# Retention and SwiGLU on one core: the second gate and val tile ahead of group 1's first pair, and the opening ordered anew

## The chip, the cores and the metric

The kernel runs on one core of a Trainium2 chip. The metric is device time in microseconds (us) of one execution, the median of three runs. Beside it stands one profiled execution; the rows below are read from that one, with times counted from the start of its span.

## The reference

Two steps are fused. The first is a block-wise linear attention with decay (a retention): inside a block the scores are masked by powers of a per-head factor, and between blocks a state is carried.

```python
for b in range(nb):
    intra = np.einsum('bhic,bhjc->bhij', qb, kb) * Dmask[None]
    intra = np.einsum('bhij,bhjd->bhid', intra, vb)
    inter = np.einsum('bhid,bhde->bhie', qb * lam_pow[None], kv_state)
    out[:, :, sl] = intra + inter
    kv_state = lam_block[None, :, None, None] * kv_state + np.einsum('bhsd,bhse->bhde', kb_dec, vb)
...
rms = np.sqrt(np.mean(x * x, axis=-1, keepdims=True) + 1e-06)
xn = x / rms * rms_g
g = xn @ w_gate
silu = g * (1.0 / (1.0 + np.exp(-g)))
return silu * (xn @ w_val) @ w_out
```

There are 4 batches of 768 tokens, 8 heads of 64, a model width of 512 and a hidden width of 1536, all in float32.

## The kernel before

**Tiling.** The 3072 tokens are cut into six groups of 512. A group's eight heads are four pairs; `Pair(m, p)` is pair p of group m. The 1536 hidden columns are twelve tiles of 128; `Hidden(m, f)` is group m's work on hidden tile f, and `Weights(f)` prepares the weights of that tile: the gate and val columns are loaded as 64-bit integers (`raw_gv`, 1 MB a tile), turned into float32 on ScalarE and VectorE (`lift`, `convert`), squared and summed for a scale (`square`, `norm`, `scale`), and split into a high and a low float16 half (`high`, `low`). The output rows of a tile come as `raw_o` (0.5 MB) by `lift_o` and `convert_o`. A gate or val product is twelve matmuls of 128x512: four of high weights by high x, four of low weights by high x, four of high weights by low x, and they can be issued a third at a time (`gate(0)`, `gate(1)`, `gate(2)`).

**The opening.** `ramp()` is a list of steps written out by hand. It runs group 0's and group 1's pairs (`p00` to `p13`), prepares weights `w0` to `w6` and does `h0` to `h5`, the first half of group 0's hidden tiles. Each engine works through its instructions in exactly the order in which the list issues them, and waits at the head of its queue for what an instruction needs. After `ramp()` a loop of units with a fixed pattern does the rest; it is the same before and after.

**What the steps are.** For a pair: `scores` (tile `pa`), `decay_a` (VectorE, the mask), `decay_k` (ScalarE), `decay_q` (GpSimd), `state_sums` (`pst`), `states`, `mix_chunks` and `mix_states` (both into `po`), `keep_output` (into `x`) and `keep_squares`. `row_sums` (`pss`) adds a group's squares; then `Norm` does `mean` (VectorE), `root` (GpSimd), `spread` (TensorE, tile `pr`), and for each quarter of the model width `scaled` (VectorE, tile `xn`), `high` (ScalarE) and `low`. The first gate matmul needs `high(0)` and the fourth `high(3)`. `busy(n)` issues n filler matmuls that nothing reads. `powers` makes the decay masks and, before the change, the powers `pw` by scans on VectorE.

**The loads.** All loads but one are issued by the sync engine (SP), in the order of the list `pending`, one entry for each `load_next()`. Pair tiles and gate-and-val tiles share four buffers (tag `in`), all four taken at first by `qkv_0_0` to `qkv_0_3`; weight tile 0 has a place of its own (`partial`). A load waits until a buffer is free. The gate and the val products have one accumulator each (`pg`, `pv`), which pairs of group 1 use too; a product can't begin until the last reader of what stood there is done.

Of the kernel before, what the change touches and what calls it, by code (L numbers as in the profile page):

```python
# [23 lines left out]
def retention_swiglu_kernel(  # L24
# [67 lines left out]
    def load_gv(f):  # L92
        if f == 0:

            t = partial.bitcast(I32).rearrange("p a (b w) -> p (a b) w", w=2)
            t = t.rearrange("p (k o) w -> p k o w", k=2)
            for i in range(2):
                nc.sync.dma_start(t[:, i], w_all[f, :, i])
        else:
            t = stage.tile([P, 2, G, 2], I32, tag="in", name=f"raw_gv_{f}", bufs=4)  # L100
            nc.sync.dma_start(t, w_all[f, :, 0:2])
            if f <= 2:
                load_o(f - 1)
        raws[f] = t
# [12 lines left out]
    pending = [(load_qkv, 1, 0), (load_gv, 1)]  # L117
# [37 lines left out]
    def powers(p, part):  # L155
        if part < 2:
            h = 2 * p + part
            nc.vector.tensor_tensor_scan(
                mask[:, h, :], lam_b[:, h : h + 1].broadcast_to([P, P]), ident, 0.0,
                ALU.mult, ALU.add,  # L160
            )
        else:
            nc.vector.tensor_tensor_scan(
                pw[:, p, :], lam_p[:, p : p + 1].broadcast_to([P, P]), zeros, 1.0,
                ALU.mult, ALU.add,
            )
# [23 lines left out]
    def scales_of(pmax):  # L190
        nc.vector.tensor_reduce(gmax, pmax[:, :P], axis=mybir.AxisListType.X, op=ALU.max)
        nc.vector.tensor_single_scalar(ge, gmax.bitcast(I32), 0x7F800000, op=ALU.bitwise_and)
        nc.vector.tensor_scalar_min(ge, ge, float(252 * EXP))
        nc.vector.tensor_scalar(sx.bitcast(I32), ge, -1.0, float(253 * EXP), ALU.mult, ALU.add)
        nc.vector.tensor_scalar(gs, gcol, sx, XS, ALU.mult, ALU.mult)
        nc.vector.tensor_scalar_add(cx.bitcast(I32), ge, float(EXP))
        nc.vector.tensor_scalar_mul(cx, cx, 1.0 / (XS * WS))
# [15 lines left out]

    zeros = wg[:, NF - 1, 1].bitcast(F32)[:, :P]
    nc.scalar.mul(zeros, ones, 0.0)
# [142 lines left out]
    class Weights:  # L358
# [79 lines left out]
        def undo(self):  # L438
            inv = small.tile([P, 2], F32, tag="inv", name=f"inv_{self.f}")
            nc.vector.tensor_scalar_add(inv.bitcast(I32), self.e2, float(64 * EXP))  # L440
            nc.vector.tensor_scalar_mul(cg[:, self.f, :], inv, cx)
# [19 lines left out]
    class Pair:  # L461
# [48 lines left out]
        def states(self):  # L510
            m, p = self.m, self.p
            for c in range(GC):
# [4 lines left out]
                if g % SEQ_CH == 0:  # L517
                    nc.vector.tensor_copy(new, self.pst[:, c, :])
                else:
# [298 lines left out]
    def ramp():  # L818
# [5 lines left out]
        powers(0, 0)  # L824
        largest()
        powers(0, 1)
        powers(2, 0)
        busy(2, 3)
        powers(2, 1)
        busy(4)  # L830
        powers(1, 2)
        powers(3, 1)
        powers(1, 0)
        powers(1, 1)
        p00.decay_k()
        pm = scales()
        p00.scores()
        powers(0, 2)
        p00.decay_q(nc.gpsimd)
        busy(5)  # L840
        p00.decay_a()
        p00.state_sums()
        p01.decay_k()
        powers(3, 0)
        p01.scores()
        p00.states()
        p01.decay_a()
        p00.mix_chunks()
        p01.state_sums()
        p01.decay_q(nc.gpsimd)  # L850
        p01.mix_chunks()
        p01.states()
        p02.scores()
        p00.mix_states()
        powers(2, 2)
        p01.mix_states()
        powers(3, 2)
        load_next()
        p02.decay_k()
        p00.keep_squares()  # L860
        p00.keep_output(nc.scalar)
        p02.decay_a()
        p03.scores()
        scales_of(pm)
        p03.decay_k()
        p01.keep_output(nc.scalar)
        row_sums(0, 0)
        p03.state_sums()
        p03.decay_q(nc.gpsimd)
        p02.decay_q(nc.gpsimd)  # L870
# [3 lines left out]
        p03.states()  # L874
        p01.keep_squares()
        p03.mix_chunks()
        w0.lift()
        p02.states()
        p02.mix_states()
        p02.keep_squares()  # L880
        w0.convert(part=0)
        w0.convert(part=1)
        p03.mix_states()
        p02.keep_output(nc.vector)
        row_sums(0, 1)
        load_next()
        p03.keep_squares()
        row_sums(0, 2)
        load_next()
        load_next()  # L890
        row_sums(0, 3)
        p03.keep_output(nc.scalar)
        w0.square(0)
        w0.square(1)
        w1.lift(0)
        w1.lift(1)
# [3 lines left out]
        p10.scores()  # L900
        p10.decay_a()
        busy(2, 3)
        w0.pn = w1.pn = ps_out.tile([P, DM], F32, tag="po3", name="pn_0")
        w0.norm()
        w1.convert(0)
        p10.decay_k()
        w1.square(0)
        n0.spread()
        w0.scale()
        w1.convert(1)  # L910
        w0.high(0)
        w1.square(1)
        n0.scaled(0)
        n0.high(0)
        p10.state_sums()
        busy(2, 1)
        w1.pn = w0.pn[:, 2:]
        w1.norm(slice(0, 1))
        w1.scale(slice(0, 1))
        n0.scaled(1)  # L920
        w0.high(1)
        n0.high(1)
        p10.states()
        n0.scaled(2)
        n0.high(2)
        p10.mix_chunks()
        load_next()
        n0.scaled(3)
        busy(2, 3)
        n0.low(1, nc.vector)  # L930
        w0.low(0)
        n0.low(2, nc.vector)
        n0.high(3)
        n0.low(3, nc.vector)
        w0.lift_o()
        w1.high(0)
        w0.low(1)
        w0.undo()
        w1.low(0)
        busy(2, 3)  # L940
# [3 lines left out]
        p10.decay_q(nc.gpsimd)  # L944
        p10.mix_states()
        p10.keep_output(nc.scalar)
        h0.gate(0)
        h0.val(0)
        h0.gate(1)
        n0.low(0, nc.gpsimd)  # L950
        h0.gate(2)
        h0.val(1)
        h0.val(2)
        w2.lift()
        h0.silu()
        w2.convert(part=0)
        h1.gate(0)
        w1.undo()
        h0.mul()
        h1.gate(1)  # L960
        w3.lift()
        w1.high(1)
        h1.gate(2)
        w2.convert(part=1)
        w1.low(1)
        w2.square(0)
        w2.square(1)
        h1.val(0)
        h1.val(1)
        w3.convert(part=0)  # L970
        w0.convert_o()
        p10.keep_squares()
        h1.silu()
        w2.pn = ps_att.tile([P, 2, G], F32, tag="ps", name="pn_2")[:, 0]
        w2.norm()
        load_next()
        w2.scale()
        w2.high(0)
        p11.decay_k()
        w2.high(1)  # L980
        h1.val(2)
        p11.scores()
        h2.gate(0)
        w3.convert(part=1)
        w2.low(0)
        high_o(0)
        w2.undo()
        h1.mul()
        h2.gate(1)
        w1.lift_o()  # L990
        w2.low(1)
        h2.gate(2)
        h2.val(0)
        h2.val(1)
        h2.val(2)
        w3.square(0)
        h0.high()
        w1.convert_o()
        h0.low()
        low_o(0, nc.vector)  # L1000
        h0.out(3)
        p11.decay_a()
        high_o(1)
        h2.silu()
        h2.mul()
        w3.square(1)
        load_next()
        p12.decay_k()
        h0.out(2)
        p11.decay_q(nc.vector)  # L1010
        w3.pn = ps_att.tile([P, 2, G], F32, tag="ps", name="pn_3")[:, 0]
        w3.norm()
        w3.scale()
        w2.lift_o()
        h1.high()
        p11.state_sums()
        p11.states()
        w2.convert_o()
        w3.high(1)
        w3.high(0)  # L1020
        p11.mix_chunks()
        w4.lift()
        load_next()
        w3.low(0)
        w3.low(1)
        p12.scores()
        p11.mix_states()
        h3.gate(0)
        high_o(2)
        w3.undo()  # L1030
        w4.convert(part=0)
        h3.gate(1)
        h0.out(0)
        h1.low()
        h3.gate(2)
        p12.decay_q(nc.vector)
        w4.convert(part=1)
        p11.keep_squares()
        p11.keep_output(nc.scalar)
        low_o(1, nc.gpsimd)  # L1040
        h3.val(0)
        h1.out(2)
        h3.val(1)
        p12.decay_a()
        w3.lift_o()
        h3.val(2)
        h3.silu()
        h0.out(1)
        w4.square(0)
        w4.square(1)  # L1050
        w4.pn = ps_att.tile([P, 2, G], F32, tag="ps", name="pn_4")[:, 0]
        w4.norm()
        p11.add_squares(nc.vector)
        h3.mul()
        w4.scale()
        p12.state_sums()
        p12.states()
        p12.mix_chunks()
        p12.mix_states()
        w4.high(1)  # L1060
        load_next()
        w4.high(0)
        w4.lift_o()
        low_o(2, nc.vector)
        w4.low(1)
        w4.low(0)
        p12.keep_output(nc.vector)
        p12.keep_squares()
        w5.lift()
        p13.scores()  # L1070
        h4.gate(0)
        h1.out(0)
        p13.decay_q(nc.gpsimd)
        h2.high()
        p13.decay_k()
        w3.convert_o()
        high_o(3)
        load_next()
        h4.gate(1)
        w5.convert(part=0)  # L1080
        h1.out(1)
        h4.gate(2)
        load_next()
        w4.undo()
        h2.low()
        w5.convert(part=1)
# [254 lines left out]
```

## Time and profile before

| what | value |
|---|---|
| median of 3 runs | 676.25 us (675.94 to 676.49) |
| the profiled execution, its own time | 677.75 us |
| its span, first to last instruction | 675.9 us |
| TensorE busy | 667.7 us, 99% of the span |
| VectorE busy | 323.1 us, 48% |
| ScalarE busy | 248.3 us, 37% |
| GpSimd busy | 78.8 us, 12% |

The span is where rows are read; the 1.85 us between it and the execution's own time lie before the first and after the last instruction. The profiled execution is 1.5 us above the median, so a difference is worked out in the span and then taken from the median. The shares are means over stages that differ: in the first 95 us VectorE and ScalarE are far busier than their shares.

### The profile page before, as it was taken

The page shows a single profiled execution, that of the slowest core. Times are in us where ns is not written, and L with a number is a line of the kernel's source. Part 1 is how long each engine was busy: PE and PEld are TensorE (multiplying, and loading weights), DVE is VectorE, ACT ScalarE, POOL GpSimd, SP SyncE. Part 2 cuts the span into 40 slices and gives each one's busy share as a digit, 9 for nine tenths or more (in the row PEclk, how much of TensorE's full clock was granted, in tenths as well). Part 3 has the DMA queues.
Part 4 walks back from the last instruction along what each step waited for, and adds up shares of the span by engine and source line. Part 5 has one row for each costly group of instructions (what it writes and reads, how often), then busy time and mean ns, then how long its engine had stood idle before and what let it go on. Part 6 is the DMA issues. An engine that isn't in the chain of part 4 may idle for free.

```text
span 675.9 us, 9923 instructions
## 1 busy us (share of the span) xinstructions
PE 667.7 (99%) x4156; PEld 359.1 (53%) x4156; DVE 323.1 (48%) x575; ACT 248.3 (37%) x438; POOL 78.8 (12%) x76
## 2 busy tenths in 40 slices
PE   8998999999999999999999999999999999999997
PEld 7856665555666444554444555444465444444443
DVE  7797857777545386332812322631341462211112
ACT  3785556776425435322213222221331221211111
POOL 2200130011214303230000111000011000000000
PEclk9999999999999999999999999999999999999999
DMA  8936622541014201122001022100100000100001
GB/s 320 365 120 225 233 109 97 185 156 63 1 64 171 79 0 63 64 99 89 1 0 58 29 102 79 47 0 1 63 1 1 1 0 1 63 0 1 1 0 62
DMA packets 14299, 50.96 MB, mean 75 GB/s; under 512 B 1712, under 2 KB 1968, under 8 KB 12848
## 3 DMA queue, kind: packets, MB, share of 16 engines
q1 hardware_dynamic: 13968, 49.69, 20.2%
q8 instruction: 32, 0.52, 0.3%
q10 hardware_dynamic: 288, 0.66, 0.3%
q14 instruction: 11, 0.09, 0.0%
HBM read 44.05 MB, written 6.29 MB: 74 GB/s over the span
## 4 chain that ended last, share of the span: by engine, by line
PE 95%; DMA 2%; DVE 2%; issue 0%; ACT 0%; DVEq 0%; SPq 0%
PE pv L697 27%; PE pg L697 27%; PE acc L716 10%; PE acc L718 9%; PE acc L717 9%; PE pa L476 4%; PE po L536 3%; PE po L547 3%; PE pst L505 2%; DMA raw_gv<-in_weights_dram 1%; PE pss L600 1%; DMA cs<-in_consts_dram 0%; DVE xn L675 0%; DVE w L233 0%; PE pss L647 0%
## 5 line engine op out<-in xcount | busy, mean ns | idle before, releaser
L697 PE MATMUL pv<-x,wv 128*128 128x512 f16 x864 | 199.1, 379 | 1.9 <-ACT x L567 1.9
L697 PE MATMUL pg<-x,wg 128*128 128x512 f16 x864 | 199.9, 379 | 0.2 <-ACT x L680 0.2
L789 DVE SCALAR_TENSOR_TENSOR sg<-pv,cv,sg 128x512 f32<-128x512 f32 x54 | 40.5, 750 | 241.7 <-PE pv L697 241.7
L697 PEld LDWEIGHTS <-wv 128*128 128x128 f16 x864 | 84.3, 98 | 102.7 <-issue 3.2
L697 PEld LDWEIGHTS <-wg 128*128 128x128 f16 x864 | 82.7, 98 | 101.2 <-issue 4.9
L718 PE MATMUL acc<-wo,hh 128*128 128x512 f16 (+1 forms) x288 | 110.3, 383 | 0.0
L717 PE MATMUL acc<-wo,hh 128*128 128x512 f16 (+1 forms) x288 | 110.2, 383 | 0.0
L782 ACT ACTIVATE sg<-pg,cg 128x512 f32<-128x512 f32 x72 | 49.3, 684 | 163.4 <-PE pg L697 163.3
L799 ACT CAST hh<-sg 128x512 f16<-128x512 f32 (+1 forms) x72 | 44.5, 617 | 162.1 <-DVE sg L789 158.3
L716 PE MATMUL acc<-wo,hh 128*128 128x512 f16 x216 | 82.0, 380 | 0.0
L496 POOL TENSOR_TENSOR qkv<-qkv,pw 128x512 f32<-128x512 f32 x22 | 28.2, 1285 | 239.7 <-PE pa L476 233.9
L806 DVE TENSOR_TENSOR hh<-sg,hh 128x512 f16<-128x512 f32 x54 | 38.0, 704 | 27.4 <-ACT hh L799 27.4
L716 PEld LDWEIGHTS <-hh 128*128 128x128 f16 x216 | 21.1, 98 | 26.6 <-issue 2.8
L718 PEld LDWEIGHTS <-hh 128*128 128x128 f16 x216 | 21.1, 98 | 25.5
L717 PEld LDWEIGHTS <-hh 128*128 128x128 f16 x216 | 21.2, 98 | 23.4
L716 PE MATMUL acc<-wo,hl 128*128 128x512 f32 x72 | 32.4, 450 | 0.0
L492 DVE TENSOR_TENSOR a<-pa,mask 128x1024 f32<-128x1024 f32 x24 | 29.3, 1222 | 5.9 <-PE pa L476 5.9
L476 PE MATMUL pa<-qkv 64*128 64x128 f32 x384 | 27.9, 285 | 0.0
L476 PEld LDWEIGHTS pa<-qkv 64*128 64x128 f32 x384 | 23.3, 187 | 8.3 <-issue 6.5
L536 PE MATMUL po<-a,qkv 128*64 128x128 f32 x384 | 25.7, 275 | 0.0
L486 ACT ACTIVATE qkv<-qkv,mask 128x256 f32<-128x256 f32 x48 | 21.7, 502 | 8.8 <-DMA qkv<-in_qkv_dram 8.8
L567 ACT COPY x<-po 128x512 f32<-128x512 f32 x22 | 12.8, 580 | 28.6 <-PE po L547 28.6
(131 smaller groups left out, 598.0 us busy)
## 6 DMA issues: line engine op xcount, KB each, us to landing
qkv<-in_qkv_dram SPq DMA_DIRECT2D x47, 512.0 KB, 4.8
raw_gv<-in_weights_dram SPq DMA_DIRECT2D x11, 1024.0 KB, 7.0
raw_o<-in_weights_dram SPq DMA_DIRECT2D x12, 512.0 KB, 3.8
out_dram<-o SPq DMA_DIRECT2D x23, 256.0 KB, 2.3
partial<-in_weights_dram SPq DMA_DIRECT2D x2, 512.0 KB, 12.3
qkv<-in_qkv_dram ACTq DMA_DIRECT2D x1, 512.0 KB, 4.1
out_dram<-o SPq DMA_DIRECT2D x1, 128.0 KB, 2.1
out_dram<-o ACTq DMA_DIRECT2D x1, 128.0 KB, 1.9
```

Of the source, the lines that this page charges most:

```text
L476: nc.tensor.matmul(self.pa[:, j, c, :], self.kT[r, c, :], self.qT[r, c, :], start=True, stop=True,)
L492: nc.vector.tensor_mul(self.a, self.pa, decay.broadcast_to([P, 2, GC, P]))
L496: eng.tensor_mul(self.qT, self.qT, pw[:, p : p + 1, :].broadcast_to([P, GC, P]))
L536: nc.tensor.matmul(po[r, c, :], self.v[:, c, r], self.a[:, j, c, :], start=c == 0, stop=False, skip_group_check=True,)
L697: nc.tensor.matmul(ps, w[:, kk, :], x[:, kk, :], start=i == kk == 0, stop=i == 2 and kk == NK - 1,)
L716: nc.tensor.matmul(acc, hl[:, ts_], oh, start=first, stop=False)
L717: nc.tensor.matmul(acc, hh[:, ts_], ol, start=False, stop=False)
L718: nc.tensor.matmul(acc, hh[:, ts_], oh, start=False, stop=last)
L782: nc.scalar.activation(self.sg, self.pg, AF.Silu, scale=cg[:, self.f, 0:1])
L789: nc.vector.scalar_tensor_tensor(out, self.pv, factor, self.sg, ALU.mult, ALU.mult)
L799: nc.scalar.copy(self.hh, self.sg)
L806: nc.vector.tensor_sub(self.hl, self.sg, hh)
```

## The change

Three things change in the helpers, and then the list in `ramp()` is written in another order with these pieces.

The first is the loads. `raw_gv_1` goes ahead of `qkv_1_0`, and the first two output tiles are both issued behind `raw_gv_2`.

The second is how the powers `pw` come about: instead of four scans on VectorE, two small matmuls a pair spread the masks over the partitions (`spread_powers`), and one ScalarE operation scales them (`powers_of`). The tile of zeros for the scans goes.

The third is that some small work can be given to another engine: five of the seven operations that make the scale of x (`scales_of`) go to GpSimd, the first state of three of group 0's pairs (`first_state`) to ScalarE, and some of the `undo` steps to GpSimd.

```diff
-            if f <= 2:
-                load_o(f - 1)
+            if f == 2:
+                load_o(0)
+                load_o(1)
...
-    pending = [(load_qkv, 1, 0), (load_gv, 1)]
+    pending = [(load_gv, 1), (load_qkv, 1, 0)]
...
+    def spread_powers(p):
+
+        ps = ps_out.tile([P, DM], F32, tag="po3", name=f"pp_{p}")
+        for j, r in enumerate(heads):
+            nc.tensor.matmul(
+                ps[r, :P], ident[:, 0:1].broadcast_to([P, D]), mask[:, 2 * p + j, :], start=True, stop=True
+            )
+        return ps
+
+    def powers_of(p, ps):
+        nc.scalar.mul(pw[:, p, :], ps[:, :P], lam_p[:, p : p + 1])
...
-    zeros = wg[:, NF - 1, 1].bitcast(F32)[:, :P]
-    nc.scalar.mul(zeros, ones, 0.0)
...
+        def first_state(self, eng=nc.vector):
             m, p = self.m, self.p
+            for c in range(GC):
+                g = m * GC + c
+                if g % SEQ_CH == 0:
+                    copy = nc.scalar.copy if eng is nc.scalar else eng.tensor_copy
+                    copy(state[:, p, g % SLOTS, :], self.pst[:, c, :])
...
         n0 = Norm(0)
         n0.mean()
         n0.root()
-        p10.scores()
-        p10.decay_a()
         busy(2, 3)
```

**The loads on SP.** The rows are those of the sync engine's queue behind weight tile 0 (`partial`); `raw_gv_1` is the second gate and val tile, `qkv_1_0` group 1's first pair, `raw_o` the output tiles. Before:

```order
L98 DMA partial_96<-in_weights_dram 128x1024 x2
L86 DMA qkv_1_0_267<-in_qkv_dram 128x1024 x2
L101 DMA raw_gv_1_375<-in_weights_dram 128x2048
L109 DMA raw_o_0_377<-in_weights_dram 128x1024
L101 DMA raw_gv_2_385<-in_weights_dram 128x2048
L109 DMA raw_o_1_387<-in_weights_dram 128x1024
L86 DMA qkv_1_1_389<-in_qkv_dram 128x1024 x2
```

And in the change:

```order
L98 DMA partial_96<-in_weights_dram 128x1024 x2
L101 DMA raw_gv_1_268<-in_weights_dram 128x2048
L86 DMA qkv_1_0_280<-in_qkv_dram 128x1024 x2
L101 DMA raw_gv_2_356<-in_weights_dram 128x2048
L110 DMA raw_o_0_358<-in_weights_dram 128x1024
L110 DMA raw_o_1_360<-in_weights_dram 128x1024
L86 DMA qkv_1_1_378<-in_qkv_dram 128x1024 x2
```

`raw_gv_1` now has one megabyte less ahead of it, and `qkv_1_0` one more.

**TensorE from group 0's row sums to the first gate matmul.** `pss` are the row sums, `pn` the scale sums of the weights, `pr` the spread, `unread` the fillers, `pg` the gate accumulator. Before:

```order
L600 MATMUL pss_0_297<-ones_116,sq_0_3_379 128x128 x4
L476 MATMUL pa_1_0_410<-qkv_1_0_267 128x128 x8
L146 MATMUL unread3_421<-ident_111 128x128 x2
L412 MATMUL pn_0_424<-ssq_0_397,ones_116 128x2
L633 MATMUL pr_0_433<-ident_111,y_0_408 128x128 x4
L505 MATMUL pst_1_0_450<-qkv_1_0_267 64x64 x6
L146 MATMUL unread1_457<-ident_111 128x128 x2
L412 MATMUL pn_0_424<-ssq_1_430,ones_116 128x1
L536 MATMUL po_1_0_475<-a_1_0_419,qkv_1_0_267 64x128 x8
L146 MATMUL unread3_488<-ident_111 128x128 x2
L547 MATMUL po_1_0_475<-qkv_1_0_267,state_122 64x128 x6
L697 LDWEIGHTS wg_130
```

And in the change:

```order
L613 MATMUL pss_0_381<-ones_116,sq_0_3_390 128x128 x4
L147 MATMUL unread3_420<-ident_111 128x128 x2
L417 MATMUL pn_0_430<-ssq_0_406,ones_116 128x1
L417 MATMUL pn_0_430<-ssq_1_415,ones_116 128x1
L646 MATMUL pr_0_451<-ident_111,y_0_425 128x128 x4
L147 MATMUL unread3_460<-ident_111 128x128 x2
L481 MATMUL pa_1_0_465<-qkv_1_0_280 128x128 x8
L510 MATMUL pst_1_0_483<-qkv_1_0_280 64x64 x6
L710 LDWEIGHTS wg_130
```

Group 1's first pair now has only its scores and state sums ahead of the gate, behind the spread; its two mixes (`po_1_0`) stand later, between `h1` and `h3`. All four row sums of group 0 now stand together ahead of these rows, where before one of them was done between the pairs.

**TensorE at the very start.** `pmax` finds the largest entry of the norm's gain, `pa_0_0` and `pst_0_0` are the first pair's scores and state sums, `pp_0` the new spread of the masks. Before:

```order
L146 MATMUL unread3_149<-ident_111 128x128 x2
L146 MATMUL unread2_153<-ident_111 128x128 x4
L187 MATMUL pmax_164<-ident_111,gmax_127 128x128
L476 MATMUL pa_0_0_166<-qkv_0_0_97 128x128 x8
L146 MATMUL unread2_177<-ident_111 128x128 x5
L505 MATMUL pst_0_0_185<-qkv_0_0_97 64x64 x8
```

And in the change:

```order
L147 MATMUL unread2_146<-ident_111 128x128 x4
L193 MATMUL pmax_152<-ident_111,gmax_127 128x128
L481 MATMUL pa_0_0_158<-qkv_0_0_97 128x128 x8
L166 MATMUL pp_0_170<-mask_123,ident_111 64x128 x2
L510 MATMUL pst_0_0_177<-qkv_0_0_97 64x64 x8
L166 MATMUL pp_1_186<-mask_123,ident_111 64x128 x2
```

Eleven fillers become four; five others now stand behind the first third of `h0`'s val product.

## Rows read from the trace of the kernel before

**Rows 1.** The page's part 1: busy time, share of the span and instructions of each engine.

```profile
PE 667.7 (99%) x4156; PEld 359.1 (53%) x4156; DVE 323.1 (48%) x575; ACT 248.3 (37%) x438; POOL 78.8 (12%) x76
```

**Rows 2.** Windows: length; PE, PEld, DVE, ACT, POOL busy (x); PEclk, DMA share, GB/s.

```profile
0.00:4.00 4.00, 2.54 (x12) 2.54 (x12) 0.00 (x0) 1.69 (x3) 0.93 (x9) 1.00 0.39 118
...
32.49:95.26 62.77, 60.67 (x411) 38.35 (x409) 50.80 (x97) 41.61 (x77) 9.95 (x8) 1.00 0.52 191
```

**Rows 3.** What TensorE waited for, the longest first: total us, times, longest us.

```profile
PE pv L697 <- ACT x L567: 1.9, 1, 1.9
```

**Rows 4.** Timeline of TensorE at the start: start, us, engine, line, operation [idle before].

```profile
1.46 2.93 PE L146 MATMUL unread<-ident 128*128 128x128 f32 x12 [1.46 <-POOL one L210]
...
6.53 1.38 PE L146 MATMUL unread<-ident 128*128 128x128 f32 x10
...
8.46 1.16 PE L476 MATMUL pa<-qkv 64*128 64x128 f32 x16
```

**Rows 5.** Timeline of TensorE from group 0's row sums to val(0).

```profile
24.25 1.16 PE L476 MATMUL pa<-qkv 64*128 64x128 f32 x16
...
29.13 1.09 PE L536 MATMUL po<-a,qkv 128*64 128x128 f32 x16
30.15 1.48 PE L146 MATMUL unread<-ident 128*128 128x128 f32 x8
...
31.68 0.87 PE L547 MATMUL po<-qkv,state 64*64 64x128 f32 x12
...
33.72 1.02 PE L697 MATMUL pv<-x,wv 128*128 128x512 f16 x4
```

**Rows 6.** Timeline of VectorE around the first scaled quarter.

```profile
29.19 0.74 DVE L675 SCALAR_TENSOR_TENSOR xn<-x,gs,pr 128x512 f32<-128x512 f32 x1
29.85 0.15 DVE L419 TENSOR_SCALAR e<-pn 128x1 int32<-128x1 int32 x1
...
31.40 1.40 DVE L675 SCALAR_TENSOR_TENSOR xn<-x,gs,pr 128x512 f32<-128x512 f32 x2
```

**Rows 7.** Timeline of ScalarE from weight tile 0 to the fourth high quarter.

```profile
18.68 1.28 ACT L221 ACTIVATE w<-partial 128x1024 f32<-128x1024 f32 x1 [0.67 <-DMA partial<-in_weights_dram]
...
22.45 0.64 ACT L408 ACTIVATE junk<-w 128x512 bf16<-128x512 f32 x1
22.99 0.20 ACT L408 ACTIVATION_READ_ACCUMULATOR junk<-w 128x1 f32 x1
...
24.72 1.25 ACT L221 ACTIVATE w<-raw_gv 128x512 f32<-128x512 f32 x2 [0.78 <-DMA raw_gv<-in_weights_dram]
25.88 0.89 ACT L486 ACTIVATE qkv<-qkv,mask 128x256 f32<-128x256 f32 x2
...
28.67 0.71 ACT L430 ACTIVATE wg<-w,sc 128x512 f16<-128x512 f32 x1
...
32.17 1.27 ACT L680 CAST x<-xn 128x512 f16<-128x512 f32 x2 [0.44 <-DVE xn L675]
```

**Rows 8.** Timeline of SP: when two of the gate and val loads were issued.

```profile
15.21 0.33 SPq L101 DMA_DIRECT2D raw_gv<-in_weights_dram  x1
...
47.97 0.43 SPq L101 DMA_DIRECT2D raw_gv<-in_weights_dram  x1
```

**Rows 9.** The page's part 6: issues, KB each, median us from issue to landing.

```profile
raw_gv<-in_weights_dram SPq DMA_DIRECT2D x11, 1024.0 KB, 7.0
```

**Rows 10.** Timeline of ScalarE around TensorE's longest wait.

```profile
57.34 1.12 ACT L221 ACTIVATE w<-raw_gv 128x1024 f32<-128x1024 f32 x1 [4.16 <-DMA raw_gv<-in_weights_dram]
...
59.36 0.58 ACT L567 COPY x<-po 128x512 f32<-128x512 f32 x1
```

**Rows 11.** Timeline of GpSimd: two decays of q, and the root.

```profile
15.91 2.52 POOL L496 TENSOR_TENSOR qkv<-qkv,pw 128x512 f32<-128x512 f32 x2 [4.92 <-PE pa L476]
24.67 1.03 POOL L624 TENSOR_TENSOR y<-ms,power 128x4 f32<-128x4 f32 x1 [6.23 <-DVE ms L620]
```

**Rows 12.** Timeline of TensorE: the first matmuls behind the ramp.

```profile
95.26 2.76 PE L697 MATMUL pg<-x,wg 128*128 128x512 f16 x12
```

More of the change, by code (lines that the diff above doesn't have):

```diff
@@ L899, in ramp @@
         n0.root()
-        p10.scores()
-        p10.decay_a()
         busy(2, 3)
[L903 to L916, printed above, removed]
+        w0.pn = ps_out.tile([P, DM], F32, tag="po3", name="pn_0")
@@ L917, in ramp @@
+        w0.norm(slice(0, 1))
         w1.pn = w0.pn[:, 2:]
         w1.norm(slice(0, 1))
+        w0.norm(slice(1, 2))
+        p10.decay_k()
+        w0.scale(slice(0, 1))
+        w0.high(0)
+        w0.scale(slice(1, 2))
         w1.scale(slice(0, 1))
+        w0.high(1)
+        w0.undo(nc.vector)
+        n0.spread()
+        n0.scaled(0)
         n0.scaled(1)
-        w0.high(1)
+        busy(2, 3)
+        n0.scaled(2)
+        p10.scores()
+        n0.high(0)
+        n0.low(0, nc.gpsimd)
@@ L937, in ramp @@
[L937 to L940, printed above, removed]
+        h0.gate(0)
+        h0.val(0)
+        busy(5)
+        w1.square(1)
+        h0.gate(1)
+        w2.lift()
+        n0.low(3, nc.vector)
+        h0.gate(2)
         w1.pn = ps_att.tile([P, 2, G], F32, tag="ps", name="pn_1")[:, 0]
         w1.norm(slice(1, 2))
[L943 to L948 removed]
@@ L949, in ramp @@
[L949 to L952, printed above, removed]
-        h0.val(2)
[L954 to L958, printed above, removed]
-        h0.mul()
[L960 to L965, printed above, removed]
+        h0.silu()
+        w0.lift_o()
+        h0.val(1)
+        w2.convert(part=0)
+        w1.low(0)
+        w2.convert(part=1)
+        load_next()
@@ L976, in ramp @@
+        w1.lift_o()
+        w1.low(1)
+        w2.high(0)
+        w2.low(0)
+        h1.silu()
+        w3.lift()
+        h1.val(1)
+        p10.decay_q(nc.gpsimd)
+        p11.decay_k()
+        h0.high()
+        w2.high(1)
+        w2.lift_o()
+        p12.decay_k()
+        w1.convert_o()
+        w3.convert(part=0)
+        w3.convert(part=1)
         load_next()
[L977 to L980, printed above, removed]
+        h2.gate(0)
+        h2.gate(1)
         h1.val(2)
+        h0.low()
@@ L996, in ramp @@
[L996 to L1010, printed above, removed]
         w3.pn = ps_att.tile([P, 2, G], F32, tag="ps", name="pn_3")[:, 0]
         w3.norm()
+        p10.first_state(nc.vector)
         w3.scale()
-        w2.lift_o()
+        w3.undo(nc.gpsimd)
@@ L1029, in ramp @@
[L1029 to L1048, printed above, removed]
         w4.square(0)
         w4.square(1)
+        p12.decay_a()
@@ L1059, in ramp @@
+        p13.scores()
+        w4.high(0)
+        w5.convert(part=0)
+        high_o(3)
         p12.mix_states()
+        load_next()
+        p12.keep_output(nc.scalar)
+        p12.keep_squares()
+        h4.gate(0)
         w4.high(1)
+        w4.undo(nc.gpsimd)
+        p13.decay_k()
+        w4.low(0)
+        h4.gate(1)
+        h4.gate(2)
+        w5.convert(part=1)
         load_next()
-        w4.high(0)
-        w4.lift_o()
-        low_o(2, nc.vector)
+        p12.add_squares(nc.vector)
@@ L1065, in ramp @@
         w4.low(1)
[L1066 to L1086, printed above, removed]
+        p13.decay_a()
@@ L1101, in ramp @@
         p13.state_sums()
+        high_o(2)
+        w5.scale()
+        p13.first_state(nc.vector)
+        p13.states(True)
+        p13.mix_chunks()
+        w5.high(0)
+        p13.mix_states()
+        load_next()
+        w4.convert_o()
+        h5.gate(0)
+        low_o(2, nc.vector)
+        w5.undo(nc.vector)
+        p13.keep_output(nc.scalar)
+        w5.low(0)
+        w6.lift()
+        w5.high(1)
+        h0.out(2)
+        h2.high()
+        low_o(3, nc.vector)
+        h2.low()
@@ L1102, in ramp @@
+        h1.out(2)
+        h1.out(3)
+        h5.gate(1)
+        w6.convert()
+        p13.keep_squares()
+        h1.out(0)
+        h2.out(2)
+        h5.val(0)
+        p13.add_squares(nc.vector)
+        h1.out(1)
+        row_sums(1, 0)
+        w5.low(1)
+        w5.convert_o()
         h3.high()
+        h2.out(0)
         h3.low()
-        w5.scale()
-        p13.states()
-        w5.lift_o()
-        w5.high(0)
-        w5.undo()
-        w5.low(0)
-        w4.convert_o()
-        w5.high(1)
```

344 lines of the change are left out of this document (182 added, 162 removed).

## The prediction

> **What bounds the kernel now.** I read the page's busy times first: TensorE is busy 667.7 of 675.9 us [rows 1], so no more than some 8 us can be won anywhere, and only where TensorE waits, or does work that nobody needs. The windows show where that is not: from the first gate matmul at 32.49 to the end of the ramp at 95.26 TensorE is busy 60.67 of 62.77 us [rows 2], and the list of its waits has one long one there, 1.9 us before a val product [rows 3]. ScalarE's timeline explains it: the lift of a gate and val tile at 57.34 had waited 4.16 us for its load, issued at 47.97, and behind it in ScalarE's queue stood the copy of a pair's output at 59.36 that frees the accumulator `pv` [rows 8, 10]. Behind the ramp nothing changes. So the whole question is at what time TensorE reaches unit 6, which is 95.26 now [rows 12].
>
> The second loss lies between the end of group 0's row sums at 24.25 and the first third of `h0`'s val product at 33.72 [rows 5]. TensorE looks busy there, but part of it are fillers: what is waited for is the chain mean, root, spread, scaled, high. The first scaled quarter stood at 29.19 and the last two began at 31.40 [rows 6], because VectorE had to mask group 1's first pair and convert weight tile 1 ahead of them, and tile 1 had come only at 24.72 [rows 7].
>
> **The change, part by part.** I work out when the val product of `h0` begins, then add what TensorE has to do from there.
>
> *The start.* Group 0's pairs arrive one after the other, and TensorE runs without a gap from the second pair's scores at 8.46 to 24.25 [rows 4, 5]. In the change the five fillers behind the first scores go, two spreads come there, and the second pair's scores can begin at about 8.05 as I estimate. Inside the stretch the spreads of pairs 2 and 3 are added; otherwise the work is the same, one row sum only moves. The trace has no spread. From below it is four records at the pace of `po` (16 records in 1.02 us, 0.25 us), from above four at the pace of a filler (10 records in 1.38, 0.55 us) [rows 4, 5]. I take 0.3, because the shape is that of `po`: the row sums end at 24.25 - 0.4 + 0.6 = 24.4, between 24.3 and 25. The four scans that VectorE loses gain nothing there, since TensorE is what binds. The five small operations on GpSimd have no row: from below 0.15 us each, as on VectorE [rows 6], from above 1.03, as the root [rows 11]. Either way they end by about 17 us, behind two decays of 1.27 us that end near 12, and the last decay of q waits for the spread of pair 3 until about 18.3 anyway. I cost them at nothing; that slack is the cover.
>
> *The second tile.* Tile 0 landed at 18.68, and the two megabytes behind it by 24.72, which is 3.0 us each [rows 7]. With `raw_gv_1` first it lands at about 21.7. ScalarE then lifts it (1.25, to 22.95) and takes three squares of 0.83 with their reads (to 25.4). The sums `pn` follow (25.9), then VectorE has eight small operations at a pace of some 0.19 (27.4). The other branch ends sooner: mean at 24.9, root of 1.03 [rows 11], spread, 27.1. So the four scaled quarters run from 27.4 to 30.1 at 0.66 to 0.70 each [rows 6]. ScalarE meanwhile has two copies of 0.58 [rows 10], `decay_k` 0.89, two high halves of tile 0 at 0.71, and then the four quarters at some 0.55 to 0.63 [rows 7]: by durations it would end at 31.3, but instructions follow each other about 0.1 us closer than they last, so 30.7. The val product begins at 30.95 where it was 33.72: 2.8 us sooner, between 2.2 and 3.3.
>
> *What is added behind it.* Group 1's first pair has now not been mixed yet: 1.02 us for the chunks and 0.81 for the states [rows 5]. Behind the first third of val five fillers stand that are real delay, 1.38 us as ten records [rows 4]; the low halves of tile 0 on VectorE, behind the masking of that pair, would hold the gate back for part of it anyway. One more `pn` costs some 0.2. Together 3.4 us.
>
> *What goes.* The 1.9 us wait [rows 3], if it isn't replaced. Two loads could replace it. I count TensorE's work forward from 30.95 (a third of a product is 0.86): 19 thirds, the pairs' parts, 6.3 us in all, fillers and sums bring it to `h3`'s val product at about 56.3, and 6.8 us more to `h4`'s gate at 63.1. VectorE has some 13.4 us of queued work from the last scaled quarter to the end of tile 3's conversion, which frees a buffer at 43.4: `raw_gv_4` is issued there, not at 47.97. With the median of 7.0 us [rows 9] it lands at 50.4, when ScalarE comes to it; ScalarE then needs 4.9 us to reach the copy and square that free `pv`, at 55.3, so the 56.3 is met. `raw_gv_5` is issued at 53.8, behind the pair's mix, and lands at 60.8; lift and high half take 1.75, 62.6 against 63.1. Both fit, by 0.5 to 1 us. With the worst seen, 9.4 us (47.97 to 57.34), the first costs about 1.3 and the second about 1.9. I take 0.4 us for small new waits, between 0 and 1.9.
>
> *The sum.* 30.95 + (95.26 - 33.72) - 1.9 + 3.4 + 0.4 = 94.4, which is 0.9 us sooner. The profiled execution would take 677.75 - 0.9, and the median 676.25 - 0.9 = **675.3 us**, 0.13% faster. What this kernel's measurement can tell from no change is about 0.2%, 1.35 us. So the early tile and its order bring 2.8 us, the moved and added work takes 3.4, and only the end of the old wait makes the balance positive.
>
> **The clock at the start.** The twelve filler records from 1.46 took 2.93 us, 0.24 each, and the ten from 6.53 took 1.38, 0.14 each [rows 4]; the granted clock stands at 1.00 (2.4 GHz) from the first window on [rows 2], and the pace says that something held the first ones to about half. The Trainium skill, "TensorE: Matmul & The Clock Gate", part 1, says that the array's clock stands at half by default and that activity releases it; by that rule fewer fillers at the start could hold the release back, and it speaks against this change, which gives four where six stood and then waits for the gain. The sum above goes by the rows: full pace when the first scores run. If the full pace came a stretch later, it is the third rival.
>
> **The rivals.**
>
> *More is won (675.3 - 0.9 = 674.4 us).* Nothing replaces the old wait (0.4), and ScalarE's chain to the fourth quarter is 0.5 shorter, since `raw_gv_1` may land nearer 21.3 and VectorE's last quarter ends at 30.1 already. For it speaks that both loads fit at the median; against it that ScalarE's queue has no gap in that chain.
>
> *A load holds the ramp again (676.8 us).* `raw_gv_5` takes the 9.4 us of rows 8 and 10: `h4`'s gate begins at 65.0, 1.9 instead of 0.4 lost: 675.3 + 1.5. For it speaks that ScalarE has this lift ahead of the high half that the gate needs; against it that the rows show only one such load waited for so long. It decides from a landing at 61.3 on.
>
> *Full pace comes late (slower side).* Until it comes, work that took 0.14 takes 0.24: each us of it costs 0.43 us from 8.05 on, when TensorE has no slack. Coming at 10 us it costs about 0.9 and the median is 676.2. From 5.3 us of such work past 8.05, a rise near 13.4 us, it eats the 0.9 and 1.35 more, and the kernel is slower by over 0.2%; a rise at 16 us gives 678.7. For it speaks the pace in rows 4; against it that TensorE has hardly a gap from 5 us on.
>
> *The early tile is worth nothing.* If mean, root and spread ended last, tile 1's time would not matter. By the sum it ends 0.3 us later than they do, so the order alone would then give nearly the same; it moves the time by under 0.3.
>
> **How the numbers follow.** My forecast, with small deviations: 0.47. More is won: 0.24. A load holds the ramp: 0.14. Late pace: 0.10, a third of it slower by over 0.2%. What I don't see, mostly other new waits in so long a new order: 0.05. Faster by over 0.2% (under 674.9) are the second case and a quarter of the first: 0.36. Slower (over 677.6) are a third of the late pace, a quarter of the loads, where both are late, and the unseen: 0.12. The rest, 0.52, is the same. The range goes from 673.8 (a start 1 us better than the forecast, spreads at their lower bound, no wait) to 677.2 (a late load and a start 0.4 worse).
>
> **What would show it.** TensorE's timeline of the changed kernel: the row sums end near 24.4, the val product of `h0` begins near 30.95, unit 6's gate near 94.4. ScalarE's lift of tile 1 stands near 21.7 and waits for its load. TensorE's list of waits has no entry over 1 us behind 31 us; a wait of `pg` or `pv` near 56 or 63 that ScalarE's lift ends would be the load rival. Fillers or `pa` at 0.24 a record past 6 us would be the late pace. It would be wrong altogether if VectorE's queue, not ScalarE's, held the low halves back between 36 and 50 us, where by my count they are ready 1 to 2 us before TensorE comes to them.

## The result and the profile after

The changed kernel takes 678.5 us (median of 8 runs, 677.94 to 679.04), the kernel before 676.3 us beside it on the same chip (median of 8, 675.94 to 677.66). The ratio is 1.0027, with a 95% interval from 1.0015 to 1.0040: slower, by some 2 us, where 675.3 us and a range of 673.8 to 677.2 were forecast.

The profiled execution has 678.52 us and a span of 676.5 us. The first part of its page stands beside [rows 1]: TensorE has ten instructions more and is busy 1.1 us longer, VectorE 4.9 us less.

```profile
PE 668.8 (99%) x4166; PEld 359.9 (53%) x4166; DVE 318.2 (47%) x561; ACT 250.0 (37%) x445; POOL 81.2 (12%) x87
```

What TensorE waited for, the longest first, is the answer to [rows 3]:

```profile
PE unread L147 <- POOL ident masks.py:199: 1.5, 1, 1.5
PE pmax L193 <- DVE gmax L186: 1.1, 1, 1.1
PE pg L710 <- ACT x L693: 0.6, 2, 0.3
PE pg L710 <- DVE x L696: 0.2, 1, 0.2
```

The 1.9 us wait of `pv` for ScalarE is gone, and no load has taken its place. So the ramp lost its one long wait and still became longer. Where that went is in TensorE's timeline, which answers to [rows 4], [rows 5] and [rows 12]:

```profile
4.67 0.80 PE L193 MATMUL pmax<-ident,gmax 128*128 128x128 f32 x2 [1.14 <-DVE gmax L186]
5.39 2.08 PE L481 MATMUL pa<-qkv 64*128 64x128 f32 x16
...
9.31 1.57 PE L481 MATMUL pa<-qkv 64*128 64x128 f32 x16
...
11.73 0.39 PE L166 MATMUL pp<-mask,ident 128*64 128x128 f32 x4
11.95 0.64 PE L510 MATMUL pst<-qkv 128*64 128x64 f32 x16
...
21.69 3.84 PE L613 MATMUL pss<-ones,sq 128*128 128x128 f32 x32
25.36 1.38 PE L147 MATMUL unread<-ident 128*128 128x128 f32 x8
26.89 0.80 PE L417 MATMUL pn<-ssq,ones 128*128 128x1 f32 x6
...
32.53 1.02 PE L710 MATMUL pv<-x,wv 128*128 128x512 f16 x4
33.39 1.28 PE L147 MATMUL unread<-ident 128*128 128x128 f32 x10
34.51 1.67 PE L710 MATMUL pg<-x,wg 128*128 128x512 f16 x7
36.34 0.38 PE L710 MATMUL pg<-x,wg 128*128 128x512 f16 x1 [0.17 <-DVE x L696]
...
65.24 2.76 PE L710 MATMUL pg<-x,wg 128*128 128x512 f16 x12
...
95.94 2.76 PE L710 MATMUL pg<-x,wg 128*128 128x512 f16 x12
```

Read it from above. The sixteen score matmuls of the first pair take 2.08 us, 0.13 us each; those of later pairs take 1.16, as `pa` in [rows 4]. So TensorE is at half pace there and still for part of the second pair's scores, which begin at 9.31 instead of the forecast 8.05. The row sums end at 25.36 (forecast 24.4). Then four fillers (eight records) hold TensorE until 26.7 and `pn` begins at 26.89. `h0`'s val product begins at 32.53 (forecast 30.95), and unit 6's gate at 95.94 (forecast 94.4): from val to unit 6 it is 63.41 us, where the forecast had 94.4 - 30.95 = 63.45. All of the 1.5 us by which the profiled execution misses its own forecast of 675.0 us of span lies ahead of the val product.

The chain behind `pn` and the two loads, in the timelines of VectorE and ScalarE (they answer to [rows 6], [rows 7] and [rows 10]):

```profile
27.73 0.16 DVE L424 TENSOR_SCALAR e<-pn 128x1 int32<-128x1 int32 x1 [2.00 <-PE pn L417]
...
28.90 1.40 DVE L688 SCALAR_TENSOR_TENSOR xn<-x,gs,pr 128x512 f32<-128x512 f32 x2
```

```profile
22.30 1.25 ACT L226 ACTIVATE w<-raw_gv 128x512 f32<-128x512 f32 x2
...
25.48 0.19 ACT L413 ACTIVATION_READ_ACCUMULATOR junk<-w 128x1 f32 x1
...
53.63 1.17 ACT L226 ACTIVATE w<-raw_gv 128x1024 f32<-128x1024 f32 x1 [1.03 <-DMA raw_gv<-in_weights_dram]
63.42 1.15 ACT L226 ACTIVATE w<-raw_gv 128x1024 f32<-128x1024 f32 x1 [3.26 <-DMA raw_gv<-in_weights_dram]
64.48 0.70 ACT L435 ACTIVATE wg<-w,sc 128x512 f16<-128x512 f32 x1
```

Tile 1 is there when ScalarE comes to it at 22.30 (no wait), and the last square is read at 25.67, near the forecast 25.4. VectorE then waits 2.00 us for `pn`, which the squares no longer hold back but the fillers do. The loads of tiles 4 and 5 make ScalarE wait 1.03 and 3.26 us, and none of it reaches TensorE. For tile 5 that is close: the high half behind its lift ends at 65.18, and the gate that needs it begins at 65.24.

### The profile page after: what moved, and what is told of

It reads as the page before. It is cut to its first block, busy times and chain, and to the rows that moved or that the text cites. A ratio compares the mean times of both kernels' runs of the same rounds, so it can differ in the third digit from the quotient of the medians.

```text
span 676.5 us, 9951 instructions
## 1 busy us (share of the span) xinstructions
PE 668.8 (99%) x4166; PEld 359.9 (53%) x4166; DVE 318.2 (47%) x561; ACT 250.0 (37%) x445; POOL 81.2 (12%) x87
## 4 chain that ended last, share of the span: by engine, by line
PE 95%; DVE 2%; DMA 2%; ACT 1%; issue 0%; SPq 0%; DVEq 0%; ACTq 0%
PE pv L710 27%; PE pg L710 27%; PE acc L729 10%; PE acc L731 9%; PE acc L730 9%; PE pa L481 4%; PE po L549 3%; PE po L560 3%; PE pst L510 2%; DMA raw_gv<-in_weights_dram 1%; PE pss L613 1%; DMA cs<-in_consts_dram 0%; DVE xn L688 0%; DVE wg L439 0%; PE pn L417 0%; PE pss L660 0%
```

## The experiments

Each kernel was timed in five rounds beside the kernel before on the same chip, unless the text says otherwise; the medians of before beside the three sets of runs were 676.42, 676.15 and 676.32 us. Every execution also has its span, which lies 1.7 to 2.1 us under its time in most of them, and up to 3.1 in some of the changed kernel and its variants; where runs fall into groups I give spans, since they show it best. The spans of the changed kernel are 676.2 to 676.7, median 676.4. The changed kernel itself was not timed again in these sets, so a difference from its 678.5 or 676.4 us goes across sets. The intervals of the ratios of its variants with one filler edit overlap its own (1.0015 to 1.0040), and what such an edit did rests on spans and profiles more than on these medians.

My theory after the result had three parts: the pace of TensorE at the start, the four fillers ahead of `pn`, and a base that was too long since the execution profiled before (span 675.9) was not a typical one. The rivals were the five fillers behind val, the load order, and plain scatter.

**The kernel before once more.** No edit.

> The kernel before, unchanged. Theory (the profiled execution of before had a wait that most executions lack): most executions have spans near 674.3 us and times near 676.2, and a profile without the 1.9 us wait of a val product on ScalarE's copy; where the wait is there, the span is near 675.9. Rival (the wait is always there, and the time outside the span differs): spans stay at 675.9 and times at 676.2.

676.8 us (675.48 to 678.75, 12 runs), ratio 0.9999 (0.9987 to 1.0012). The spans go from 673.5 to 676.8 with a median of 674.85. The profiled execution is a long one, 676.8: its first `pa` takes 2.08 us, as in the changed kernel, and the wait of `pv` is 1.14.

```profile
5.41 2.08 PE L476 MATMUL pa<-qkv 64*128 64x128 f32 x16
...
10.63 1.16 PE L476 MATMUL pa<-qkv 64*128 64x128 f32 x16
...
60.98 1.02 PE L697 MATMUL pv<-x,wv 128*128 128x512 f16 x4 [1.14 <-ACT x L567]
```

So even with six fillers the pace comes late in some executions, and the 1.9 us are no constant. Late pace costs the kernel before as well: the second pair's scores begin 2.17 us later than in [rows 4].

**Six fillers at the start of the changed kernel.**

```diff
         powers(2)
-        busy(4)
+        busy(6)
         largest()
```

> The changed kernel with six fillers at the start instead of four, so that TensorE works until about 4.4 us as in the kernel before. Theory (fewer fillers let full pace come late): the first scores take about 1.1 us instead of 2.1, the row sums end near 24.4 instead of 25.4, and the time falls by 1.0 to 1.4 us, to about 677.3. Rival (full pace comes when it comes, whatever the fillers): the first scores still take 2.1 us and the time stays at 678.5.

677.98 us (676.66 to 679.04, 12), ratio 1.0020 (1.0009 to 1.0031). Eight spans lie at 674.9 to 675.4, median 675.15, and four at 676.6 to 677.2. The profiled one is of the first group:

```profile
5.20 1.73 PE L481 MATMUL pa<-qkv 64*128 64x128 f32 x16
...
8.27 1.16 PE L481 MATMUL pa<-qkv 64*128 64x128 f32 x16
...
23.91 1.38 PE L147 MATMUL unread<-ident 128*128 128x128 f32 x8
...
31.09 1.02 PE L710 MATMUL pv<-x,wv 128*128 128x512 f16 x4
```

The second pair's scores begin 1.04 us sooner than in the changed kernel, the val product 1.44. Two thirds of the executions win 676.4 - 675.15 = 1.25 us, the others nothing; in the median time it is 0.5. With four fillers none of eight executions was in the short group. No execution of the long group was profiled, so that late pace makes it is argued. Two of these four list a mean granted clock of 0.998; of all other executions only those with the old load order, below, list one under 0.999. So a fall of the clock further on is a rival for them.

**No filler ahead of `pn`.**

```diff
-        busy(2, 3)
         n0 = Norm(0)
         n0.mean()
         n0.root()
-        busy(2, 3)
```

> The changed kernel without the four fillers between group 0's row sums and the sums pn. Theory (they hold pn back by a microsecond, and pn is what the scaled quarters wait for through VectorE's small operations): pn begins near 25.8 instead of 26.9, the val product of h0 near 31.6 instead of 32.5, the time falls by about 0.9 to 677.6. Rival (root and spread end last anyway, or TensorE falls back to half pace in the gap): the time stays within 0.3 of 678.5 or rises.

677.39 us (676.52 to 678.19, 12), ratio 1.0012 (1.0003 to 1.0022): 1.1 us in the medians, 676.4 - 675.6 = 0.8 in the spans.

```profile
25.09 0.98 PE L417 MATMUL pn<-ssq,ones 128*128 128x1 f32 x6
26.63 1.16 PE L646 MATMUL pr<-ident,y 128*128 128x128 f32 x8 [0.56 <-POOL y L637]
...
31.46 1.02 PE L710 MATMUL pv<-x,wv 128*128 128x512 f16 x4
```

`pn` begins 1.80 us sooner, val 1.07: the rest is lost where `pr` now waits for the root on GpSimd, which is the next to be late. Of the 1.07 us, 0.27 come from the start of this execution, since its row sums end at 25.09 and not at 25.36; 0.8 are left, as in the spans. The four fillers were on the path, and the forecast had left them out.

**No filler behind val.**

```diff
         h0.val(0)
-        busy(5)
         w1.square(1)
```

> The changed kernel without the five fillers behind the first third of h0's val product. The prediction's sum took them as 1.38 us of delay: by that the time falls by about 1.3, to 677.2. Theory now (the gate waits for the last low quarter of x, which VectorE ends at 36.3 whatever TensorE does): the last third of h0's gate ends at the same time, and the time stays within 0.3 of 678.5.

677.91 us (677.38 to 678.97, 12), ratio 1.0019 (1.0008 to 1.0030); median span 676.1.

```profile
31.53 1.02 PE L710 MATMUL pv<-x,wv 128*128 128x512 f16 x4
33.48 1.69 PE L710 MATMUL pg<-x,wg 128*128 128x512 f16 x7 [0.92 <-DVE wg L439]
35.34 0.38 PE L710 MATMUL pg<-x,wg 128*128 128x512 f16 x1 [0.18 <-DVE x L696]
```

Without the fillers TensorE waits 0.92 us for the low half of tile 0 instead, and the last held third of the gate begins 35.34 - 31.53 = 3.81 us after val. In the changed kernel it is 36.34 - 32.53 = 3.81. From val to unit 6, which begins at 94.97, it is 63.44 us against 63.41. So in the profiles the fillers cost nothing; VectorE sets that time. The medians alone would not show it: the span is 0.3 us shorter, which the expectation allowed, but the time is 0.6 shorter, which it did not. The profiled execution is the shortest of the twelve, and what it gains lies ahead of the edit: its second scores begin at 8.71 and its row sums end at 24.36.

**Four fillers in the kernel before.**

```diff
-        busy(2, 3)
         powers(2, 1)
         busy(4)
```

> The kernel before with four fillers at the start instead of six. Theory (fewer fillers let full pace come late, in most executions): the first scores take about 2.1 us in the profile, val of h0 begins near 35.5 instead of 33.7, and the median rises by 1.2 to 2.0 us, to about 678. Rival (when full pace comes is chance, the fillers change nothing): the median stays within 0.5 of 676.4.

676.86 us (676.08 to 677.75, 11), ratio 1.0011 (1.0002 to 1.0020): 0.7 us, between theory and rival. The profile (span 674.9) shows one way in which it can be less than in the changed kernel:

```profile
4.96 2.08 PE L476 MATMUL pa<-qkv 64*128 64x128 f32 x16
...
34.43 1.02 PE L697 MATMUL pv<-x,wv 128*128 128x512 f16 x4
...
59.05 1.02 PE L697 MATMUL pv<-x,wv 128*128 128x512 f16 x4 [0.24 <-ACT x L567]
...
94.30 2.76 PE L697 MATMUL pg<-x,wg 128*128 128x512 f16 x12
```

The pace is late and val comes 0.71 us later than in [rows 5], but the wait at the end of the ramp is 0.24 instead of 1.9, because the load landed 7.7 us after its issue and not 9.4 as in [rows 8, 10]. Unit 6 is reached 0.96 us sooner than in [rows 12]. This is one execution; whether the typical one of this version saves its late pace in that wait is not shown.

**The old load order in the changed kernel.**

```diff
-    pending = [(load_gv, 1), (load_qkv, 1, 0)]
+    pending = [(load_qkv, 1, 0), (load_gv, 1)]
```

> The changed kernel with the pair's load ahead of the second gate and val tile again, as in the kernel before; all else as changed. Theory (the order of the steps needs the early tile: squares, pn and scaled wait for it): ScalarE lifts tile 1 near 24.7 instead of 22.3, val of h0 begins about 2 us later, the time rises to about 680.3. Rival (fillers, row sums and root hide the load anyway): the time stays within 0.5 of 678.5.

680.5 us (679.68 to 681.39, 6), ratio 1.0062 (1.0047 to 1.0077). ScalarE lifts tile 1 at 24.52 after waiting 2.55 us for it, val begins at 34.23, 1.70 us later, and the time is 2.0 us longer. The early tile is worth that much in this order of steps; the fourth rival, which gave under 0.3, is out. In the profiled execution a part came by a way that nobody expected (windows of that profile; columns as in [rows 2]):

```profile
20.00:29.60 9.60, 8.12 (x78) 7.43 (x75) 5.49 (x18) 6.62 (x16) 1.38 (x2) 1.00 0.99 391
29.60:33.00 3.40, 3.40 (x27) 2.95 (x27) 3.08 (x6) 3.28 (x7) 1.53 (x2) 0.50 0.95 382
33.00:36.00 3.00, 3.00 (x29) 2.08 (x28) 3.00 (x3) 1.61 (x4) 1.98 (x2) 1.00 0.13 49
```

In the second of these rows the granted clock is 0.50 (1.2 GHz), and `pa` at 30.74 takes 2.08 us. In the row before it TensorE stood idle for 1.5 us, 1.1 of them in one wait of `pn` for ScalarE's squares. The fall alone does not make these executions long: four of the six list a mean granted clock of 0.996 or 0.997, but the shortest (span 677.6) lists 0.999 and the longest (679.0) 1.00.

**Both filler edits together** (six at the start, none ahead of `pn`).

> The changed kernel with six fillers at the start and none between the row sums and pn. Theory (late pace and fillers ahead of pn are two separate costs): their gains add, 1.0 and 0.8 us, to a median span near 674.6 and a time near 676.6, no different from the kernel before. Rival (they overlap, since root and spread end next): the time stays at 677.4 or above.

676.75 us (676.00 to 678.58, 11), ratio 1.0008 (0.9998 to 1.0017). In the profile (span 674.3) the first `pa` takes 1.16 us, the second begins at 7.87, the row sums end at 23.80, val begins at 30.18 and unit 6 at 93.70.

```profile
23.80 1.00 PE L417 MATMUL pn<-ssq,ones 128*128 128x1 f32 x6
...
30.18 1.02 PE L710 MATMUL pv<-x,wv 128*128 128x512 f16 x4
...
93.70 2.76 PE L710 MATMUL pg<-x,wg 128*128 128x512 f16 x12
```

With these fillers the forecast's course (24.4, 30.95, 94.4) is reached and beaten by 0.7 us in this execution. The median span is 675.0, 0.4 over what was expected of this run. It is just what the forecast gave its profiled execution, and the median time still does not get under before: it stands 1.45 us over the forecast 675.3. What is left over is the base.

**Chunk products in the place of the five fillers**, on top of it: `p10` is mixed in the gap behind val.

```diff
         h0.val(0)
-        busy(5)
+        p10.mix_chunks()
         w1.square(1)
...
         w2.undo(nc.gpsimd)
-        p10.mix_chunks()
         w2.convert_o()
```

> The same, and the chunk mix of group 1's first pair stands in place of the five fillers behind the first third of val, instead of later. Theory (TensorE waits there for VectorE's low quarters whatever it does, so work put there is free): another 1.0 us is won, a median span near 673.6 and a time near 675.6, faster than both kernels. Rival (TensorE, sooner by a microsecond, meets the loads of tiles 4 and 5 and waits there): the gain is under 0.4 and the profile shows the wait of a gate or val product near 60 to 65 us.

675.51 us (675.05 to 676.95, 11), ratio 0.9991 (0.9980 to 1.0001). Val begins at 30.11 and unit 6 at 92.66, 1.04 us sooner than with the fillers, which is the work that has moved into the gap. The interval just reaches no difference from before. A second time the same kernel gave less:

> The version with the chunk products in the fillers' place once more, to see whether it beats the kernel before. Theory: 675.5 as in its first runs (675.05 to 676.95), 0.5 to 0.8 us under before, ratio 0.9990. Rival (no difference from before): within 0.2 us of it.

676.13 us (674.91 to 677.21, 11), ratio 0.9994 (0.9985 to 1.0003): no difference that can be told. Its profile (span 675.0) has a new wait, since TensorE now comes to `h3`'s val product earlier than tile 4's load lets ScalarE free the accumulator:

```profile
56.90 2.75 PE L710 MATMUL pv<-x,wv 128*128 128x512 f16 x12 [1.44 <-ACT sq L591]
```

**Eight fillers there.** `busy(6)` becomes `busy(8)`.

> The same with eight fillers at the start in the place of six. Theory (the first fillers decide when TensorE has its full pace, and six leave it late in some executions): the executions with a long span (674.4 to 675.2) go and those at 673.3 to 673.7 stay, or all are 0.2 to 0.4 us longer since the two added fillers end at 4.6 to 4.9 us and hold the maximum's product, which began at 4.27; median 675.1 to 675.7. Rival (the pace rises at a time that the fillers do not set): spans in two groups as with six, median up by 0.2 to 0.5.

676.15 us (675.29 to 676.99, 11), ratio 0.9995 (0.9986 to 1.0004), spans from 673.5 to 675.2 without a gap between groups: two more fillers win nothing. The profile has the full pace (`pa` 1.16) and the same 1.5 us wait of `pv`, so it is rather the load that spreads these spans; that was only argued.

**One load issued earlier in the kernel before.** The test of the base: the wait is taken away and nothing else is changed.

```diff
         h0.high()
+        load_next()
         w1.convert_o()
...
         w3.square(1)
-        load_next()
         p12.decay_k()
```

> The kernel before, with nothing changed but the place of one load: that of tile 4's gate and val is issued ahead of w1.convert_o(), so that it no longer stands on SyncE's queue behind tile 1's out load. In the profile of before it was issued at 47.97 us and landed 9.4 us later, and the wait of the val product for ScalarE (1.9 us) stood behind that landing; the buffer is free at about 44.2, so it should be issued there and land by about 53.5 even at 9.4 us, ahead of the 53.2 to 57.3 at which ScalarE asked for it. Theory (the 1.9 us wait belongs to the long execution that was profiled and is small in the median one): the time falls by 0.2 to 0.9 us only, ratio 0.9987 to 0.9997. Rival (the wait is as long in the typical execution, and the base of the sum was sound): it falls by about 1.9 us, to 674.3, ratio 0.997.

675.62 us (675.41 to 675.86, 11), ratio 0.9983 (0.9973 to 0.9992). Its 11 spans lie between 673.5 and 674.0, where the 27 of before beside them go from 673.3 to 676.7 with a median of 674.4. In its profile (span 673.6) tile 4's load is issued at 43.73 and ScalarE lifts it at 52.86 without a wait.

```profile
52.86 1.15 ACT L221 ACTIVATE w<-raw_gv 128x1024 f32<-128x1024 f32 x1
```

```profile
92.96 2.76 PE L697 MATMUL pg<-x,wg 128*128 128x512 f16 x12
```

These are all waits of TensorE but the first one:

```profile
PE pg L697 <- ACT x L680: 0.2, 1, 0.2
```

Against the execution of [rows 12] unit 6 begins 95.26 - 92.96 = 2.30 us sooner and the span is 2.3 us shorter, as the rival wanted. Against the median of before it is 0.7 us by the medians and 1.1 by the ratio, whose interval makes it 0.5 to 1.8. So the wait is worth 1.9 us in that one execution and some 0.7 to 1.1 in the typical one. One thing stays open: spans that lie within 0.5 us leave no room for late pace, though the edit stands behind the start and late pace began the second scores 2.17 us later in the profile of the first experiment. Eleven good starts may be luck, and then a part of the gain is theirs. This version beats both kernels, by some 0.1 to 0.2% in one set of runs, and it is the one to keep.

**The kernel before a third time**, a single profiled execution.

> One look at the kernel before, unchanged, to see what a second execution of it spends in the val product's wait. Theory (the wait varies with the landing of tile 4's load, and a typical execution has a span of 674.2 to 674.5): at a span of 674.0 to 674.8 the wait is under 1.0 us and the load lands in under 8.5 us. Rival (the wait is part of every execution): 1.9 us again, and a shorter span comes from elsewhere.

It was neither of the two: the execution took 679.13 us, a span of 677.2, with late pace (`pa` 2.08 us) and a wait of 1.33.

```profile
58.72 1.13 ACT L221 ACTIVATE w<-raw_gv 128x1024 f32<-128x1024 f32 x1 [3.58 <-DMA raw_gv<-in_weights_dram]
```

Issued at 49.93, the load took 8.8 us. All three executions of before that were profiled (675.9, 676.8, 677.2) lie in the upper part of its spans. The last two had late pace and the first had the longest wait; why no typical one was profiled stays open. It makes the point on the base stronger, not weaker, and it means that no profile shows the wait of a typical execution of before: what the base is off by rests on the early load's version.

## Why the prediction was wrong

**"The sum", its base: the term of -1.9 us was mis-sized.** The wait stood in the one profiled execution, 677.75 us, and the gain was subtracted from the median, 676.25, which has less of it. The early load shows about 0.7 us for it at the median (1.1 by the ratio, interval 0.5 to 1.8) in place of 1.9. That is 1.2 (or 0.8) of the 3.2 us between 675.3 and 678.5. The 1.5 us between the two numbers stood in the table of times and should have been the warning: an execution that is 1.5 us over the median holds losses that the median does not.

**"The start": full pace when the first scores run. This step failed**, and the third rival's mechanism is what happened. The second pair's scores began at 9.31 in place of 8.05, the row sums ended at 25.36 in place of 24.4: 0.96 us, close to the 0.9 that the rival gave for a late pace. That closeness is partly luck. The scores were 1.26 us late and the second pair's took 0.41 longer (1.57 in place of 1.16); but from the second scores to the end of the row sums the forecast had 24.4 - 8.05 = 16.35, and without the 0.41 it took 15.64, as it did with six fillers (8.27 to 23.91). So the slow start cost about 1.7 us, and 0.7 of it came back. The rival counted the cost only from 8.05 on; but TensorE waited for nothing between the first and the second scores, so what was lost ahead of 8.05 counted too. Six fillers in place of four bring back 1.25 us of span in two thirds of the executions. The late pace had a chance of 0.10, which was too little. By the rival's own price it would have made 676.2 us and not 678.5, so it alone does not account for the time. The Trainium skill, "TensorE: Matmul & The Clock Gate", part 1, says that the same kernel's slow start varies from run to run. The traces agree: in three profiles of the kernel before the first `pa` took 1.18 us once and 2.08 twice. In all kernels with six fillers at the start it took 1.16, 1.18, 1.73 or 2.08 us, with four 2.08 in all five profiles. The spreads of pairs 2 and 3 held TensorE 0.22 us each from their start to the next one (11.73 to 11.95), where the sum had 0.3, and were not the cause.

**"The second tile": the tile was right, "the sums `pn` follow (25.9)" failed.** Tile 1 was lifted at 22.30 without a wait and the squares ended 0.3 us from the forecast, but four fillers stood on TensorE's queue between the row sums and `pn`; the step did not count them. Taking them out gave 0.8 to 1.1 us. The forecast's 2.8 us were for the early tile and the order of steps together; the tile alone, taken back, cost 2.0.

**"What is added behind it": the size was right and the owner wrong.** The five fillers' 1.38 us are not a delay of theirs: by the profile without them TensorE waits for the low halves on VectorE, and the gate's last third comes after the same 3.81 us. The forecast named that cover and still booked the fillers as real. From val to unit 6 it was 63.41 us against 63.45.

**"What goes": the loads.** Both fitted at TensorE (no wait in the profile after; 0.17 to 0.45 us in four of the experiments), so the second rival is out for the changed kernel. Tile 5's fitted by 0.06 us where the forecast had 0.5: it was issued at 56.07 in place of 53.8 and lifted at 63.42 in place of 60.8, and the gate came at 65.24 in place of 63.1. The 0.4 us for small new waits was not needed; that the way from val to unit 6 still came out to 0.04 us is luck in part, since something of that size, which no run singles out, took its place. In the version with the chunk products the first of these loads does hold TensorE, for 1.4 us.

**GpSimd's five small operations** took 0.19 to 0.28 us each and ended at 15.0: hidden, as forecast.

**Added up.** By the profiles the 3.2 us are 1.5 of the course up to val, 0.2 outside the span (2.0 us where it was 1.85) and 1.5 of base: the profiled execution of before stood 1.5 us over its median, the profiled one after stands at its own. In the course the slow start (about 1.7) and the fillers ahead of `pn` (0.8) stand against 0.9 that the forecast had counted too long. Of the base's 1.5 the early load accounts for 0.8 to 1.2, only within its interval, and the rest is not assigned. That the two costs of the course add was shown by the run that has both edits.

## What to carry to other kernels

A gain read from one profiled execution is to be taken from that execution's own time, and before it is taken from the median, ask whether the wait belongs to the typical one: a wait that ends on a load scatters with the load. On the path between two products count every instruction on the queue, fillers first, and try to put real work where they stand. And where a change takes work away from the start, price the late pace as a case of its own, since where differences are under half a per cent it can decide the sign.

## What the runs showed of the hardware

The full pace of TensorE begins at a different time in executions of one and the same kernel: the sixteen `pa` of the first pair took 1.18 us in one profile of before and 2.08 in two others. The granted clock of the first windows reads 1.00 although their matmuls run at half pace ([rows 2] and [rows 4]), so at the start the pace must be taken from durations; only a later fall, as in the old load order, shows in that column. And the 1 MB load of tile 4, the same bytes from the same place in the program, took 7.7, 8.6, 8.8 and 9.4 us from issue to ScalarE's lift in four executions with the order of before.
